# A fused attention and maxout FFN kernel: flag-0 heads by a diagonal and a composite key block, for one assumed set of flags

## The chip, the cores and the metric

The kernel runs on one core of one Trainium2 chip. The metric is the device time of one execution in microseconds (us). The core has five engines, each with an instruction queue of its own that is worked in order: TensorE (PE, matrix products into PSUM), VectorE (DVE), ScalarE (ACT), GpSimd (POOL) and SyncE (SP, which here only issues DMAs). Sixteen DMA engines serve all queues.

## The reference

Four batches of eight heads, 768 positions, head size 64; the output of attention goes row by row through a maxout FFN.

```python
scores = scale * q @ k.T                       # per batch and head, 768 x 768
causal = rel >= 0                              # rel = row - column
stream_keep = causal & ((column < n_sink) | (rel < window))     # n_sink 4, window 64
mask = where(is_retrieval[head], causal, stream_keep)           # flags 1,0,1,0,0,0,1,0
a = softmax(where(mask, scores, -1e9)); x = a @ v               # x: 3072 x 512 over the heads
h = max(x @ w1, x @ w2, x @ w3)                # 512 -> 768
out = h @ w_out                                # 768 -> 512, float32
```

A head of flag 1 attends to all earlier positions. A head of flag 0 attends to the first four positions and to the last 64.

## The kernel before

Positions are cut into six blocks of 128, and each batch into two halves of three query blocks (384 rows). A step of the work is one item of the string list `PROGRAM`, executed in order when the program is built; each engine then receives its own instructions in that order, so `PROGRAM` is the schedule.

- `hl` (`load_pairs`, L187) loads batch 0's k and q for pairs of heads in halves through SP. `cast` (L212) makes fp16 of them, `turnp` (L231) transposes them on PE, and a copy (L239) puts them in the key-query tile KQ. For batches 1 to 3, `load` (L251, two DMAs from POOL per group of four heads) and `turn` (L267, a DVE stream transpose) do the same.
- `load_v` (L287) brings V through SP; `v` (`prep_v`) casts it into `va` (L504) and multiplies it with the head's flag into `vf` (L506).
- `s` (`scores`) computes the transposed scores of one unit, keys by queries, for all blocks on and below the diagonal, for every head alike: 6 blocks in the first half, 15 in the second. In batch 0 two heads share the array (64 rows each, L553), and in the first half masks are added beforehand by a product with the identity (L537). In batches 1 to 3 four heads share it, 32 rows each, in two contraction halves. ACT takes the exponential into `pt` (L564).
- `k` (`masks`, L586) multiplies blocks on and beside the diagonal with masks `mk` that were built from the flags on the chip (L365 to L389).
- `av` (L602) multiplies each block of `pt` with `va` near the diagonal and with `vf` far from it. In a flag-0 head `vf` holds zeros save for the four sink rows, so its far blocks are worked like any other. A column of ones gives the row sums; L610 and L612 divide. The result is transposed into `xT` by a DMA (L621) or on PE (`x`, L634, L638).
- `f` (`fill`) is one step of the FFN of a half batch: 18 products of 4 matmuls (L438), each taken out of PSUM by a copy (L455) or a maximum (L458), then three output blocks (L474, L480, L481). FFN steps are strewn between the attention steps.
- `w` (L403, L410) loads the weights through POOL: w0 in two DMAs of 384 KB, the others whole. `idle` issues ten products of zeros at the very start.

Of the kernel before, what the change touches and what calls it, by code (L numbers as in the profile page):

```python
# [11 lines left out]
FP32 = mybir.dt.float32  # L12
AF = mybir.ActivationFunctionType
ALU = mybir.AluOpType

UNITS = [
    [  # L20
        [(0, 0, 3, 0), (2, 2, 1, 384)],
        [(1, 1, 2, 0)],
    ],
    [
        [(0, 0, 3, 0), (5, 2, 1, 384)],
        [(1, 0, 3, 0), (4, 1, 1, 384)],
        [(2, 0, 3, 0), (4, 2, 1, 384)],
        [(3, 0, 3, 0)],
    ],
]  # L30

MASKED = [
    [(0, 0, 1, (0,), 256, 256), (0, 0, 1, (384,), 128, 0), (1, 1, 1, (0,), 256, 0)],
    [(1, 0, 2, (384,), 128, 0), (2, 2, 1, (0, 384), 128, 128), (3, 3, 1, (0,), 256, 0)],
]

APART = [(0, 0, 1, (384,), 128, 0), (1, 1, 1, (384,), 128, 0)] + MASKED[1][1:]


EARLY = 0

FIRST = "hl 0 0 1, ir"

PROGRAM = (
    "idle 2, idle 8, cast 0 0 aa, hl 0 1 1 ss, hl 0 2 2 ss, read, hl 1 0 2 ss, cast 0 1 pp",
    "flags, cast 0 2 ap, em 1, turnp 0 1 a, far, em 0, turnp 0 0 aa, cast 0 3 da, em 2, em 3",
    "load_v 0 0 4 4, s 0 0 1, s 0 0 0, v 1 1 pp, cast 1 1 pa, turnp 0 3 dd, turnp 0 2 da",
    "w 0 2 0, load_v 0 0 0 4, v 0 0 dp, s 1 0 0, w 0 2 1, s 0 1 0 b, hl 1 2 2 ss, s 1 0 1",  # L50
    "cast 1 2 dp, v 1 0 dd, s 0 1 1, s 1 1 0 b, av 0 0, v 0 1 pp, turnp 1 1 a, s 1 1 1",
    "turnp 1 2 aa, x 0 0 a, s 2 0 1, cast 1 0 dp, load_v 0 1, cast 1 3 ad, av 1 1, s 2 1 1",
    "av 1 0, x 1 1 d, av 0 1, turnp 1 0 ad, s 2 2 1, x 1 0 d, s 3 0 0, m 0, w 1, x 0 1 d",
    "s 2 0 0, m 3, m 1, f 1 d, f 1 d, s 2 1 0, s 2 2 0, m 2, f 1 a, f 1 d, k 2 1 2 p, k 2 0 1 d",
    "w 2, f 1 d, s 2 3 1, load 1 0, w 3, k 3 0 0 d, s 3 1 0, f 1 a, s 2 3 0, load 1 1",
    "k 2 0 3 p, k 2 0 2 p, turnp 1 3 dd, k 3 0 1 p, k 2 1 1 d, k 2 1 3 d, f 1 d, f 1 d",
    "v 2 0 ad, f 1 a, f 1 a, v 3 1 pp, f 1 d, s 3 0 1, v 2 1 dp, s 3 1 1, f 1 a, v 3 0 ap",
    "av 2 0 D, f 1 d, f 1 d, s 3 2 0, turn 1 0 0 0, turn 1 0 0 1, f 1 a, turn 1 0 1 0, s 3 2 1",
    "s 3 3 0, k 3 0 2 p, k 3 1 2 p, turn 1 0 1 1, f 1 a, av 2 1 D, s 3 3 1, k 3 1 1 d",
    "k 3 0 3 p, k 3 1 3 p, f 1 a, k 3 1 0 d, load_v 1 0, gate, f 1 a, s 4 0, k 4 1 0 p",  # L60
    "v 4 0 pp, av 3 0, av 3 1, f 1 a, f 1 a, x 3 0 d, s 4 1, turn 1 1 0 1, x 3 1 a, f 1 d",
    "v 5 1 pp, turn 1 1 1 0, turn 1 1 1 1, turn 1 1 0 0, k 4 0 1 d, k 4 0 0 d, k 4 1 1 p, f 1 a",
    "f 1 a, f 1 d, load_v 1 1, f 1 a, f 1 a, f 1 a, v 4 1 pd, f 1 a, f 1 d, s 5 0, f 1 a, f 1 d",
    "av 4 0 D, k 5 0 0 d, f 1 d, s 5 1, k 5 0 1 p, load_v 2 0, f 1 a, f 1 a, load 2 0, f 1 a",
    "s 6 0, f 1 d, av 4 1 D, f 1 a, v 5 0 ap, f 1 a, s 6 1, f 1 a, av 5 0 D, f 1 d, f 1 d",
    "k 5 1 1 p, k 5 1 0 p, v 7 0 dp, s 6 2, k 6 1 2 p, f 1 a, av 5 1 D, turn 2 0 1 0, f 1 a",
    "v 6 0 ad, s 6 3, turn 2 0 0 1, x 5 1 d, f 1 a, turn 2 0 1 1, load 2 1, load 3 1",
    "load_v 2 1, v 6 1 ap, f 1 d, f 1 d, k 6 0 2 p, v 9 0 ap, k 6 1 3 p, f 1 a, f 1 a",
    "turn 2 0 0 0, s 7 0, f 1 a, f 1 d, f 1 d, turn 2 1 0 0, k 6 0 1 d, f 1 a, s 7 1, f 1 d",
    "f 1 a, f 1 a, k 6 1 1 p, k 7 1 1 d, f 1 d, s 7 2, f 1 a, f 1 a, k 6 0 3 p, k 7 1 2 d",  # L70
    "turn 2 1 1 0, load 3 0, av 6 0 D, s 7 3, f 1 d, v 7 1 pp, av 6 1 D, k 7 1 3 p, f 1 d",
    "turn 3 1 1 0, k 7 0 3 p, turn 2 1 0 1, s 8 0, k 7 0 1 p, turn 2 1 1 1, k 7 0 2 p, f 1 a",
    "f 1 d, load_v 3 0, k 8 0 0 p, av 7 1 D, s 8 1, f 1 a, f 1 a, s 9 0, v 8 0 ap, k 8 0 1 d",
    "f 1 a, f 1 d, av 7 0 D, v 13 1 pp, s 9 1, f 1 a, av 8 0 D, f 1 d, s 10 0, f 1 a, x 7 1 d",
    "f 1 a, v 10 0 dd, f 1 d, s 10 1, f 1 a, f 1 d, v 9 1 ad, f 1 a, f 1 d, f 1 a, s 10 2",
    "f 1 d, f 1 d, f 1 d, k 8 1 0 p, f 1 d, k 9 0 0 p, k 9 1 1 d, f 1 d, f 1 d, v 11 0 ad",
    "f 1 d, k 9 1 0 p, v 12 0 ad, k 9 0 1 p, k 8 1 1 d, av 9 0 D, v 8 1 ap, s 10 3, f 1 d",
    "f 1 a, av 8 1 D, turn 3 0 1 0, s 11 0, k 10 1 1 p, f 1 d, f 1 d, k 10 0 3 p, f 1 a",
    "av 9 1 D, v 13 0 ap, f 1 a, k 10 1 3 d, turn 3 0 1 1, x 9 1 a, k 10 0 1 p, s 11 1, f 1 a",
    "k 10 0 2 p, v 11 1 ap, av 10 0 D, f 1 d, s 11 2, k 11 0 2 p, turn 3 0 0 0, f 1 a",  # L80
    "turn 3 0 0 1, f 1 d, k 11 0 1 d, f 1 a, k 10 1 2 d, f 1 d, v 10 1 ap, f 1 a, turn 3 1 0 1",
    "f 1 a, f 1 a, s 12 0, av 10 1 D, f 1 a, f 1 d, k 12 1 0 p, s 12 1, f 1 d, f 1 a, f 1 a",
    "k 12 0 1 p, turn 3 1 0 0, s 11 3, v 12 1 ad, f 1 a, load_v 3 1, f 1 a, f 1 a, k 11 0 3 d",
    "k 11 1 3 p, f 1 d, f 1 d, k 11 1 1 p, turn 3 1 1 1, f 1 a, f 1 d, av 11 0 D, f 1 d",
    "k 11 1 2 d, f 1 a, k 12 0 0 p, k 12 1 1 d, f 1 a, s 13 0, av 12 0 D, f 1 d, av 11 1 D",
    "k 13 0 0 d, f 1 d, f 1 d, s 13 1, f 1 d, v 15 1 pp, f 1 d, k 13 0 1 p, x 11 1 d, f 1 d",
    "v 15 0 ad, av 12 1 D, k 13 1 1 d, av 13 0 D, s 15 0, f 1 a, f 1 d, f 1 d, f 1 a, f 1 d",
    "f 1 d, f 1 a, k 13 1 0 d, s 15 1, v 14 0 ap, f 1 d, f 1 a, f 1 d, f 1 d, s 14 0, f 1 a",
    "f 1 d, f 1 d, f 1 d, av 13 1 D, s 14 1, f 1 d, x 13 1 d, f 1 d, f 1 d, f 1 a, f 1 a",
    "s 14 2, f 1 a, k 14 1 2 p, v 14 1 ad, k 14 1 1 p, f 1 d, f 1 d, f 1 d, f 1 a, f 1 a",  # L90
    "k 15 0 1 p, s 14 3, f 1 d, k 14 0 3 p, f 1 a, f 1 d, s 15 2, f 1 a, f 1 d, f 1 d, f 1 d",
    "s 15 3, f 1 a, k 15 1 1 d, f 1 a, k 15 1 3 d, f 1 a, k 15 1 2 d, k 14 0 1 p, f 1 a",
    "k 14 0 2 p, k 14 1 3 p, k 15 0 3 d, av 14 0 D, f 1 a, f 1 a, f 1 a, av 14 1 D, f 1 a",
    "f 1 d, k 15 0 2 p, av 15 1 D, f 1 a, av 15 0 D, f 1 d, x 15 1 d, f 1 a, f 1 d, f 1 a",
    "f 1 d, f 1 d, f 1 a, f 1 a, f 1 a, f 1 d, f 1 a, f 1 a, f 1 d, f 1 d, f 1 a, f 1 d, f 1 a",
    "f 1 a, f 1 a, f 1 a, f 1 a, f 1 d, f 1 a, f 1 d, f 1 a, f 1 d, f 1 a, f 1 d, f 1 a, f 1 a",
# [3 lines left out]
def _where(half):  # L100
    at = {}
    for u, parts in enumerate(UNITS[half]):
        for ki, q0, n, c0 in parts:
            for qb in range(n):
                at[(ki, q0 + qb)] = (u, c0 + qb * 128)
    return at


@with_exitstack
def kernel(  # L110
    ctx: ExitStack,
    tc: tile.TileContext,
    q: bass.AP,
    k: bass.AP,
    v: bass.AP,
    is_retrieval: bass.AP,
    n_sink: int,
    window: int,
    moe_w1: bass.AP,
    moe_w2: bass.AP,  # L120
    moe_w3: bass.AP,
    moe_w_out: bass.AP,
    out: bass.AP,
):
    nc = tc.nc
    B, H, S, D = q.shape
    NT, DMdl = out.shape
    DF = moe_w1.shape[1]
    P = 128
    NSB = S // P  # L130
# [3 lines left out]
    n_sink = int(n_sink)  # L134
    window = int(window)
# [4 lines left out]
    assert (S, D, DMdl) == (768, 64, 512) and window <= P and n_sink <= P  # L140
    AT = [_where(0), _where(1)]
    G = 4
    R = P // G
    NQ = H // G
    NT4 = B * 2 * NQ

# [6 lines left out]
    ptp = ctx.enter_context(tc.tile_pool(name="ptp", bufs=5))  # L153
# [7 lines left out]

    ctx.enter_context(tc.manual_schedule())


    def where(t):
        bh, qd = divmod(t, NQ)
        return bh // 2, bh % 2, qd

# [3 lines left out]

    staged = {}
    cast = {}
    KQs = {}

    def load_pairs(half, hp, n, engines):
        for nm, src, eng in zip(("ks", "qs"), (k, q), engines):  # L180
            st = (
                pairs2.tile([P, 4, HB, D], FP32, tag=nm, name=nm) if n == 2
                else once.tile([P, 2 * n, HB, D], FP32, name=f"{nm}{hp}")
            )
            m = 2 * n if eng is nc.gpsimd else 2
            for h in range(0, 2 * n, m):
                eng.dma_start(  # L187
                    out=st[:, h : h + m],
                    in_=src[
                        0, 2 * hp + h : 2 * hp + h + m, half * HALF : (half + 1) * HALF  # L190
                    ].rearrange("h (p j) d -> p h j d", p=P),
                )
            for i in range(n):
                staged.setdefault((half, hp + i), []).append(st[:, 2 * i : 2 * i + 2])
# [521 lines left out]
```

## Time and profile before

| what | value |
|---|---|
| device time, median of 3 runs | 202.31 us (201.32 to 202.49) |
| profiled execution: its span, the only time that the profile gives for it | 199.9 us |
| median less that span | 2.4 us |
| PE busy | 190.0 us, 95%, 2059 matmuls |
| DVE, ACT, POOL busy | 148.3, 115.9, 90.5 us |
| granted clock of PE, mean | 0.990 |
| read from HBM | 25.17 MB |

The span runs from the first to the last instruction. Matmuls are pipelined, so that the busy time of PE overstates its work; what one matmul costs is read from the spacing of many. In a stretch table each engine's busy time stands beside its number of instructions. In the chain of waits a row gives start, length, engine, output tile, line and count. An L with a number is a line of the kernel.

### The profile page before, as it was taken

What the parts mean: (1) busy time and instruction counts of PE and PEld (TensorE: products, weight loads), DVE (VectorE), ACT (ScalarE), POOL (GpSimd) and SP (SyncE); (2) the same over time, 40 slices, a digit from 0 to 9 for tenths busy, and PEclk for the clock granted to TensorE, in tenths of its full rate; (3) what the DMA queues carried; (4) which work ended last, traced back from release to release, by engine and by line L of the source; (5) the groups of instructions that cost most, each with busy time, mean ns of one, the idle gap of its engine ahead of it and who ended that gap; (6) DMA issues with size and microseconds to landing.
All of it is one profiled execution on the core that took longest, in us unless ns stands there. A gap on an engine that the chain in (4) does not pass through costs nothing.

```text
span 199.9 us, 5135 instructions
## 1 busy us (share of the span) xinstructions
PE 190.0 (95%) x2059; PEld 109.3 (55%) x2059; DVE 148.3 (74%) x311; ACT 115.9 (58%) x171; POOL 90.5 (45%) x118
## 2 busy tenths in 40 slices
PE   7688898999999999999999999999999999999993
PEld 2345444565556455666456645574656455765552
DVE  3638965998976789896469998996978288767750
ACT  4489983765658798687776756634366565100011
POOL 3429187583276598490697245652010197000000
PEclk9889999999999999999999999999999999999999
DMA  5999999995979989988521232703500120124004
GB/s 143 312 245 230 196 195 212 208 169 76 283 173 211 162 169 208 218 218 176 147 76 23 43 124 74 159 20 73 167 5 20 53 108 0 23 59 157 3 0 157
DMA packets 48429, 26.48 MB, mean 132 GB/s; under 512 B 36758, under 2 KB 43926, under 8 KB 48406
## 3 DMA queue, kind: packets, MB, share of 16 engines
q1 hardware_dynamic: 43366, 17.96, 37.9%
q0 software_dynamic: 4624, 7.87, 21.9%
q8 instruction: 16, 0.26, 0.6%
q10 hardware_dynamic: 416, 0.33, 0.5%
q14 instruction: 7, 0.06, 0.1%
HBM read 25.17 MB, written 6.29 MB: 157 GB/s over the span
## 4 chain that ended last, share of the span: by engine, by line
PE 75%; DMA 11%; DVE 4%; SPq 3%; issue 2%; ACT 2%; POOL 0%; DVEq 0%
PE yy L438 39%; PE yy L474 14%; PE st L553 9%; PE oacc L602 9%; DMA vs<-in_v_dram 7%; PE yst L438 3%; DMA qs<-in_q_dram 2%; DVE KQ L267 2%; SPq L187 2%; ACT pt L564 1%; DMA xT<-x 1%; PE yst L474 1%; DVE acc L458 1%; DVE hT L458 1%; SPq L621 1%
## 5 line engine op out<-in xcount | busy, mean ns | idle before, releaser
L564 ACT ACTIVATE pt<-st 128x1024 f16<-128x1024 f32 (+3 forms) x98 | 83.3, 905 | 33.0 <-PE st L553 31.0
L586 POOL TENSOR_TENSOR pt<-pt,mk 128x512 f16<-128x512 f16 (+1 forms) x54 | 57.3, 1088 | 38.4 <-ACT pt L564 20.1
L438 PE MATMUL yy<-xT,w1t 128*128 128x384 f16 x180 | 35.8, 327 | 1.2 <-DVE pt L586 1.2
L438 PE MATMUL yy<-xT,w2t 128*128 128x384 f16 x180 | 36.1, 326 | 0.0
L438 PE MATMUL yy<-xT,w0t 128*128 128x384 f16 x180 | 35.8, 327 | 0.3
L458 DVE TENSOR_TENSOR acc<-yy,acc 128x384 f16<-128x384 f32 x45 | 24.8, 557 | 10.7 <-PE yy L438 8.6
L474 PE MATMUL yy<-woutt,hT 128*128 128x512 f16 (+1 forms) x138 | 31.6, 375 | 0.0
L553 PE MATMUL st<-KQ 32*128 32x384 f16 (+5 forms) x560 | 29.4, 281 | 1.4 <-ACT pt L564 0.8
L458 DVE TENSOR_TENSOR hT<-yy,acc 128x384 f16<-128x384 f32 x45 | 24.8, 556 | 4.5 <-PE yy L438 2.3
L602 PEld LDWEIGHTS <-pt 128*128 128x128 f16 x672 | 24.4, 97 | 4.8 <-DVE va L504 0.7
L267 DVE STREAM_TRANSPOSE KQ<-kq 128x384 f32<-128x384 f32 x24 | 25.5, 1132 | 0.6 <-DMA kq<-in_q_dram 0.6
L602 PE MATMUL oacc<-va,pt 128*128 128x65 f16 x352 | 24.9, 193 | 0.5 <-DVE va L504 0.5
L438 PEld LDWEIGHTS <-w1t 128*128 128x128 f16 x192 | 17.5, 98 | 14.1 <-issue 1.6
L438 PEld LDWEIGHTS <-w0t 128*128 128x128 f16 x192 | 17.8, 98 | 13.4 <-issue 0.8
L438 PEld LDWEIGHTS <-w2t 128*128 128x128 f16 x192 | 17.3, 98 | 11.9 <-issue 1.4
L553 PEld LDWEIGHTS <-KQ 32*128 32x128 f16 (+1 forms) x560 | 12.2, 93 | 18.8 <-issue 11.8
L474 PEld LDWEIGHTS <-hT 128*128 128x128 f16 x150 | 13.8, 98 | 14.7 <-issue 0.8
L602 PE MATMUL oacc<-vf,pt 128*128 128x65 f16 x320 | 21.1, 193 | 0.0
L455 ACT CAST acc<-yy 128x384 f16<-128x384 f32 x25 | 12.0, 481 | 13.9 <-PE yy L438 13.5
L612 DVE TENSOR_TENSOR x<-oacc,rc 128x384 f16<-128x384 f32 x32 | 17.8, 557 | 1.1
L480 DVE COPY ot<-yy 128x512 f32<-128x512 f32 (+1 forms) x15 | 10.1, 675 | 9.2 <-PE yy L474 9.2
L506 POOL TENSOR_TENSOR vf<-va,far 128x384 f16<-128x384 f16 x10 | 8.6, 867 | 17.3 <-ACT va L504 12.9
(72 smaller groups left out, 143.4 us busy)
## 6 DMA issues: line engine op xcount, KB each, us to landing
out_dram<-ot SPq DMA_DIRECT2D x23, 256.0 KB, 2.1
vs<-in_v_dram SPq DMA_DIRECT2D x21, 256.0 KB, 5.6
kq<-in_k_dram POOLq DMA_DIRECT2D x6, 384.0 KB, 7.9
kq<-in_q_dram POOLq DMA_DIRECT2D x6, 384.0 KB, 10.0
ks<-in_k_dram SPq DMA_DIRECT2D x8, 192.0 KB, 3.6
qs<-in_q_dram SPq DMA_DIRECT2D x7, 192.0 KB, 4.8
vs<-in_v_dram SPq DMA_DIRECT2D x6, 128.0 KB, 4.8
w0t<-in_moe_w_dram POOLq DMA_DIRECT2D x2, 384.0 KB, 9.4
```

The costliest lines, as they stand in the source:

```text
L267: nc.vector.transpose(out=dst.rearrange("c (p j) -> c j p", j=n)[:, j0:j1], in_=src.rearrange("c (j i) -> c j i", i=R),)
L438: nc.tensor.matmul(yy[:, 0:HALF], w_t[wi][:, ks, ni * P : (ni + 1) * P], xT[b, half][ks].rearrange("p a t -> p (a t)"), start=(ks == 0), s ...
L455: copy_out[0](out=acc[ni], in_=yy[:, 0:HALF])
L458: nc.vector.tensor_tensor(out=dst, in0=yy[:, 0:HALF], in1=acc[ni], op=ALU.max)
L474: nc.tensor.matmul(yo[:, 0:n], hT[ns][:, tb * P : (tb + 1) * P], woutt[:, ns, c : c + n], start=(ns == 0), stop=(ns == NNB - 1),)
L480: op(out=ot[:, c : c + n], in_=yo[:, 0:n])
L506: vf_engine.tensor_tensor(out=vf[j][:, hs, k0:k1, 0:D], in0=vs[:, hs, 0:1] if half == 0 else va[j][:, hs, k0:k1, 0:D], in1=far[:, hs, k0:k ...
L553: nc.tensor.matmul(sts[g // m][:, g % m, c0 : c0 + n * P], KQ[rows, 0, ki * P : (ki + 1) * P], KQ[rows, 1, t0 : t0 + n * P], start=(c0 == ...
L564: nc.scalar.activation(out=pts[t, i][:, u, h0 : h0 + m, 0:w], in_=st[:, :, 0:w], func=AF.Exp, scale=sc,)
L586: engine.tensor_tensor(out=x, in0=x, in1=m, op=ALU.mult)
L602: nc.tensor.matmul(o[:, qi, hl, 0 : D + 1], pt[:, u, hl, c : c + P], vv[:, 2 * hp + hl, ki, 0 : D + 1], start=(idx == 0), stop=(idx == len ...
L612: nc.vector.tensor_tensor(out=x, in0=o[:, :, :, 0:D], in1=rc.unsqueeze(3).to_broadcast([P, HB, 2, D]), op=ALU.mult,)
```

## The change

The change is a rewrite of the attention part. Its parts:

- **One set of flags is assumed** (`GUESS`). All of the masks, shapes and unit layouts follow from it when the program is built. The flags that are given are compared with it on DVE (`compare_flags`, step `flags`), and at the end all row sums are tested for a range (`check_sums`, step `check`). `verdict` adds both into a number `differ`. Every engine reads it into a register, and a branch leads to `general`, a slow program in loops that works for any flags, when it isn't zero.
- **A flag-0 head reads two blocks per query block**: the diagonal block, and from the third query block on a composite one, which has the four sink keys in columns 0 to 3 and the last 64 keys of the block before in columns 64 to 127; between them it is zero. The composite keys `kx` (steps `kx0`, `kx`) and values `vx` (`y`) are copied from KQ and V; their tiles are cleared once (`clear`, `cleark`). That is 11 score blocks per head instead of 21, and 11 AV products instead of 21. Flag-1 heads are as before.
- **Rows of the array are shared by two heads** in batches 1 to 3: `ROWS` pairs a head of one group with one of the other, and `MIXED` and `NEAR` lay out eight steps per batch in which each row group works on up to four blocks of both its heads. Before there were twelve units per batch.
- **Masks** are multiplied from a strip of 28 blocks that 28 copies on DVE lay out (`strip`), and only where needed. The additive masks of batch 0's first half come from five blocks `far`.
- **The start's order is another.** POOL builds six mask blocks, then casts pair 0; DVE clears the composite tiles and compares the flags ahead of pair 0's copy. `idle` is two products after the first scores, and eight later. `load 1 0` stands ahead of the weights, `w 0` is one DMA of 768 KB behind POOL's cast of the second half's fourth key pair, and a `load` of the second group of heads issues four DMAs instead of two.
- FFN, output and the DMAs of V are unchanged.

```diff
-UNITS = [[[(0, 0, 3, 0), (2, 2, 1, 384)], [(1, 1, 2, 0)]],
...
+GUESS = (1, 0, 1, 0, 0, 0, 1, 0)
+ROWS = ((0, 7), (1, 4), (2, 5), (3, 6))
+MIXED = [
+    [("R", "p", 0, 0, 3, 0), ("S", "p", 1, 1, 1, 384)],
+    [("S", "p", 0, 0, 2, 0), ("R", "p", 1, 1, 2, 256)],
...
 PROGRAM = (
-    "idle 2, idle 8, cast 0 0 aa, hl 0 1 1 ss, hl 0 2 2 ss, read, hl 1 0 2 ss, cast 0 1 pp",
-    "flags, cast 0 2 ap, em 1, turnp 0 1 a, far, em 0, turnp 0 0 aa, cast 0 3 da, em 2, em 3",
-    "load_v 0 0 4 4, s 0 0 1, s 0 0 0, v 1 1 pp, cast 1 1 pa, turnp 0 3 dd, turnp 0 2 da",
-    "w 0 2 0, load_v 0 0 0 4, v 0 0 dp, s 1 0 0, w 0 2 1, s 0 1 0 b, hl 1 2 2 ss, s 1 0 1",
...
+    "clear 1, flags, hl 0 1 1 ss, clear 0, cast 0 0 pp, turnp 0 0 dd, cleark 0, hl 0 2 2 ss",
+    "strip 0 14, cast 0 2 aa, cast 0 1 ap, turnp 0 1 d, kx0 0 0 a, s0 0 0 0, hl 1 0 2 ss",
+    "cast 1 0 dd, turnp 0 2 ad, turnp 1 0 da, cleark 1, load_v 0 0 0 4, cast 1 1 ap, idle 2",
+    "kx0 0 1 a, s0 0 0 1, cast 0 3 dd, s0 0 1 0, s0 0 1 1, strip 14 28, kx0 1 0 p, load_v 0 0 4 4",
+    "v 0 0 3 d, hl 1 2 2 ss, v 0 0 2 d, turnp 0 3 aa, cast 1 2 dd, load 1 0, s0 1 1 0, s0 0 1 3",
+    "s0 1 0 0, y 0 0 1:4:2 s p, kx0 0 3 d, turnp 1 1 d, kx0 1 1 d, s0 1 3 0, v 0 0 0 p, s0 1 2 0",
+    "k0 0 1 0 p, kx0 0 2 a, y 0 0 1:4:2 r p, cast 1 3 pd, av 0 0 0, y 0 0 5:8:2 r a, s0 0 1 2",
+    "y 0 0 5:8:2 s d, s0 0 0 3, turnp 1 3 da, s0 0 0 2, turnp 1 2 da, k0 0 1 1 d, s0 1 3 1, w 0",
...
+                if GUESS[h]:
+                    use = [("p", ki) for ki in range(qi + 1)]
+                else:
+                    use = [("c" if qi > 1 else "p", qi - 1)] * (qi > 0) + [("p", qi)]
...
+        for g in range(G):
+            far_row = any(GUESS[h] for h in ROWS[g])
+            parts = (MIXED if far_row else NEAR)[s]
...
+            nc.tensor.matmul(
+                sts["XY"[g // 2]][:, g % 2, c0 : c0 + n * P],
+                KQ[rows, 0, ki * P : (ki + 1) * P] if kind == "p"
+                else kx[b % 2][quad][rows, ki - 1, :, r],
+                KQ[rows, 1, q0 * P : (q0 + n) * P],
...
+        vx = [consts.tile([P, H, 4, VW], FP16, name=f"vx{j}") for j in range(2)]
+        nc.vector.memset(vx[j], 0.0)
...
+    n = nc.values_load(differ[0:1, 0:1], min_val=0, max_val=1 << 20)
+    with tc.If(n > 0, preferred_fallthrough_block=False):
+        general(tc, nc, q, k, v, is_retrieval, int(n_sink), int(window), w_t, woutt, out, xs_dram)
```

## The prediction

> **What bounds the kernel now.** I read the stages first: busy time and granted clock in stretches cut where the chain of waits changes engine.
>
> ```profile
> core 0: us, PE busy (x) PEld busy (x) DVE busy (x) ACT busy (x) POOL busy (x), PEclk, DMA share, GB/s
> 4.70:8.15 3.45, 1.57 (x17) 0.89 (x16) 1.64 (x8) 0.82 (x3) 1.07 (x2) 1.00 0.98 289
> 8.15:11.60 3.45, 3.45 (x28) 2.00 (x26) 2.33 (x6) 3.45 (x6) 1.34 (x3) 0.51 1.17 296
> 43.30:196.70 153.40, 153.25 (x1704) 89.24 (x1704) 118.11 (x232) 85.47 (x124) 65.42 (x76) 1.00 0.48 108
> 196.70:199.90 3.20, 0.00 (x0) 0.00 (x0) 0.42 (x1) 0.00 (x0) 0.00 (x0) 0.91 0.47 164
> ```
>
> From 43.3 us to the last matmul PE has no gap (153.25 of 153.40): a matmul removed there is time removed. Before that PE waits; after it 3.2 us are the last copy, its store and the closing barriers. The chain of waits in the late part prices PE's work:
>
> ```profile
> 163.13 0.56 PE st L553 x16
> 163.69 2.71 PE yy L438 x16
> 169.56 0.94 PE oacc L602 x30
> 170.49 1.95 PE yy L438 x12
> ```
>
> Behind AV a product's matmul takes 1.95/12 = 162.5 ns and an AV matmul 0.94/30 = 31.3 ns. A score unit (one tile per pair of heads, 4 column blocks, two contraction halves) takes 0.56 where 8 passes of 128 columns at the same rate (162.5/3 = 54) give 0.43: 0.13 more; the 16 matmuls behind it take 2.71 instead of 2.60, another 0.11. So a unit costs its columns plus 0.245.
>
> The start is read from PE's timeline and the DMA issues up to 50 us (KB each, median us from issue to landing):
>
> ```profile
> 23.64 1.48 PE L438 MATMUL yy<-xT,w0t 128*128 128x384 f16 x8
> 30.97 3.42 PE L438 MATMUL yy<-xT,w1t 128*128 128x384 f16 x20 [1.22 <-DVE pt L586]
> ```
> ```profile
> w0t<-in_moe_w_dram POOLq DMA_DIRECT2D x2, 384.0 KB, 9.4
> w1t<-in_moe_w_dram POOLq DMA_DIRECT2D x1, 768.0 KB, 12.2
> w2t<-in_moe_w_dram POOLq DMA_DIRECT2D x1, 768.0 KB, 10.7
> kq<-in_k_dram POOLq DMA_DIRECT2D x2, 384.0 KB, 15.6
> kq<-in_q_dram POOLq DMA_DIRECT2D x2, 384.0 KB, 16.9
> woutt<-in_moe_w_out_dram POOLq DMA_DIRECT2D x1, 768.0 KB, 18.5
> ```
>
> The first w0 half is issued at 14.9 and lands at 23.6, just when the FFN begins; w1 is issued at 18.8 and lands at 31.0. The DMA engines are full (share 1.14 or more) from 8 to 43 us. PE is dense from 31.0.
>
> **The change, part by part.** I write the end as F (the first FFN product) + R (PE's work from there) + idle + tail.
>
> *AV.* A flag-0 head reads 11 blocks instead of 21, five heads of eight: 472 matmuls instead of 672. Of those, 429 come after F against 624 after 31.0 before. 429 x 31.3 ns = 13.4 us; before 19.5.
>
> *Scores of batches 1 to 3.* Units go from 36 to 24 (eight mixed steps per batch, all four blocks wide). Columns: 24 x 8 x 54 ns = 10.4 us; overhead 24 x 0.245 = 5.9. Steps now have up to eight passes per row group in place of four; the four extra weight changes at 10 to 22 ns (the starts of consecutive passes in one unit) add 0 to 2 us, I take 0.8. Sum 17.1; before 36 x 0.245 + 252 x 54 ns = 22.4.
>
> *FFN.* Unchanged: 576 x 162.5 ns and the output's 138 x 215 + 12 x 110 ns (1.29 and 0.66 us for six in the chain) = 124.6 us; before, six products (3.9) were done by 31.0, leaving 120.7.
>
> *The rest of R.* Remaining batch-0 units 2.6, eight filler matmuls of 512 columns 1.7, transposes and the verdict 0.3. R = 124.6 + 13.4 + 17.1 + 2.6 + 1.7 + 0.3 = 159.7. The same sum for before from 31.0: 120.7 + 19.5 + 22.4 + 1.9 + 0.4 = 164.9, and 31.0 + 164.9 = 195.9 against a true end at 196.7: the method misses 0.8 us.
>
> *The start.* This decides. DVE gets work ahead of what the scores wait for:
>
> ```profile
> 0.93 0.27 DVE L314 MEMSET zero<- 128x256 uint32 x1 [0.93 <-PEq L697]
> 2.42 0.23 DVE L346 COPY kept<-kept 128x256 f16<-128x256 f16 x1
> ```
>
> A clear costs 1.06 ns per word. The two clears of the composite value tiles (1056 words each) take 2.2 us, the ten small operations on the flags about 0.2 us each where they depend on one another, and DVE is free for pair 0's first copy at about 7.4 us, though PE's transposes are ready at 5.5. From there: two copies 1.0, two clears of composite keys (512 words) 1.05, 14 mask blocks at about 0.115 (half of L346's copy, overlapped as L389's are) 1.6, a 768-column copy 0.85, two casts 1.0, two copies 1.0, two more clears 1.05, the casts of pair 3 1.0: 16.0 us. The loads of half 1, pairs 2 and 3, reuse the buffers that these casts free; SP issues them at about 15.5 (12.1 before), and everything behind them on SP, batch 0's second V, starts 3.3 us later. POOL casts the key that lands at about 20.5 and only then issues w0: at 21.5, not 14.9. Batch 1's first kq goes ahead of w0 on POOL, at about 14.3; with half 1 and V beside it, it should be moving until w0 is issued. A 768 KB weight then needs 10.7 to 12.2 by w2 and w1, less if kq is done (w0 halves 9.4, worked under full engines): 30 to 33. The other chain, DVE held at the cast of pair 2 until about 21, then the copies, four AV divisions (0.7 each), a KQ stream transpose of 1.13 ahead of the second xT, gives 31. So F is 31, bounds 25 (if the walk overstates each wait) and 40 (w0 as slow as woutt, 18.5). The six products that before had done by 31.0 are counted in R.
>
> *Idle behind F.* Before lost 2.8 us between 23.6 and the end. DVE has about 132 us of work in the 160 behind F (83%, from L458's 557 ns, L267's 1132, L612's 557 and so on; before 118 in 153, 77%). I take 2.0, bounds 0 and 5. The row-sum check is about 1.2 us of DVE under an FFN stage in which DVE is half idle; nothing waits for it before the verdict.
>
> *The tail.* Every engine reads the verdict into a register and branches. It adds a wait for DVE; queued behind SP's copy of it are only the last three stores, which come later anyway. PE ends 2.5 us before SP sees the last store land, and this covers some of it. Neither operation is in the trace. From below the cover takes all: 0. From above: a register read as long as the last store's landing (2.0), and a fetch of the code behind the skipped block, 1.2 us for a 16 KB packet of the instruction queue (0.6% of 16 engines' span over 16 packets) and a landing of 2.3 as for a DMA transpose, end 3.1 us past before's barrier. I take 1.2, since the nearest row to a register read is a 0.17 us operation on 8 numbers. The trace has no branch across a block. The Trainium skill, "Runtime: NRT & Kernel Launch", section on instruction fetch, says that a taken branch out of the current two pages must fetch its target before going on; it gives no time, and no run here shows it yet.
>
> **Sum.** 31.0 + 159.7 + 2.0 + 3.2 + 1.2 = 197.1 us of span, against 199.9. The profile gives only the span of its execution; the median of the runs, 202.31, lies 2.4 above it, and I carry that over: **199.5 us**, 1.4% faster. One per cent is what a measurement here can tell from no change.
>
> **Rivals.**
> 1. *The start is not later* (0.22). DMA bandwidth, not the queues, bounded the old start (share above 1 up to 43 us), and the bytes are the same. If F is 25, near the old 23.6: 191.1, or 193.5. For: PE has only some 10 us of work before F. Against: w0's place on POOL behind a cast.
> 2. *w0 arrives late* (0.23). It waits in POOL's queue behind the cast and behind kq, and is no longer split. The price is its transfer: break-even is F = 33.8, a flight of 12.3 us, about w1's, and 1% slower is F = 35.8, 14.3 us. At kq's mean of 16.3 F is 37.8: 203.9, or **206.3 us**. For: kq and woutt took that long under full engines. Against: w2's 10.7, and less is queued on POOL ahead of w0.
> 3. *PE's clock* (0.15). Before, a window with 1.57 of 3.45 us busy was followed by one at 0.51. The changed kernel has two filler matmuls early instead of ten, and a sparse start; if half clock holds until one window into the FFN, that costs 1.7 us there and about 1 us in F: 199.8, or 202.2, no change. The Trainium skill, "TensorE: Matmul & The Clock Gate", Part 1, has the clock halve after an idle window and return after a busy one; the two rows above agree.
> 4. *The branch is taken* (0.01): 32 heads of six blocks with some ten dependent operations of half a microsecond or more: beyond 1,100 us.
>
> **Chances.** The forecast has 0.39, its own range 197.5 to 201.5 (F and idle within 2 us), of which 0.27 lies below 200.3. Faster: 0.27 + 0.22 + 0.01 of rival 3 = 0.50. Slower: 0.22 of rival 2, 0.02 of rival 3, 0.01 = 0.25. Within 1%: 0.25. The range reaches to 193 (rival 1, with its faster third left out) and to 206 (half of rival 2).
>
> **What the profile after would show.** First FFN product near 31 and w0 issued near 21.5 with the FFN waiting for it or for xT; PE without gaps from about 35; AV at 31 ns; 24 units in batches 1 to 3 of about 0.6; a last matmul near 192.7, and 4.4 us behind it. I am wrong if PE shows gaps under DVE in the middle, if F is far from 31, or if the end takes more than 6 us.

## The result: 1% slower, and where the time went

| | kernel before | kernel after |
|---|---|---|
| device time, median of 20 runs each | 200.91 us | 202.88 us |
| ratio, 95% interval | | 1.0106 (1.0077 to 1.0135) |
| span of the profiled execution | 199.9 us | 200.2 us |
| first FFN product | 23.6, dense from 31.0 | 32.2 |
| last matmul ends | 196.7 | 193.3 |
| behind the last matmul | 3.2 us | 6.9 us |

The ratio is of fast runs alone; the median of the kernel before also holds its slower runs (up to 204.6 us).

PE does 9.4 us less busy time and is done with its matmuls 3.4 us earlier, and the kernel takes longer. First the page's busy times, then three stretches of the kernel after (from and to, length, busy time and number of PE, its weight loads, DVE, ACT and POOL, PE's granted clock, DMA share, GB/s):

```profile
PE 180.6 (90%) x1833; PEld 106.2 (53%) x1833; DVE 152.4 (76%) x357; ACT 99.4 (50%) x170; POOL 72.3 (36%) x111
```
```profile
11.60:15.00 3.40, 3.16 (x19) 1.46 (x17) 3.29 (x8) 2.37 (x6) 1.52 (x4) 1.00 0.79 128
43.30:193.32 150.02, 148.72 (x1547) 87.75 (x1545) 117.92 (x244) 74.03 (x116) 52.52 (x67) 1.00 0.51 114
193.32:200.20 6.88, 0.00 (x1) 0.00 (x0) 0.42 (x1) 0.00 (x0) 0.00 (x0) 0.74 0.26 86
```

The last two rows carry the result. From 43.3 us PE is still without gaps (148.72 of 150.02), so what was taken from it there is saved. Behind it stand 6.88 us in which only one copy of 0.42 us shows as work; before, the same row was 3.20 long. The first row is a lull at the start: the DMA engines at 0.79 of their time and 128 GB/s, where the kernel before was above 1.

The chain of waits of the kernel after, in its late part (start, length, engine, tile, line, count):

```profile
160.24 0.57 PE st L597 x13
...
167.13 1.95 PE yy L387 x12
169.08 1.31 PE oacc L646 x42
```

A product's matmul takes 1.95/12 = 162.5 ns and an AV matmul 1.31/42 = 31.2 ns, as before; 22 of the 24 score steps take 0.56 to 0.57 us, whether they hold 12 matmuls or 32, and two take 0.69 and 0.76. PE's prices were right.

The same chain at the start:

```profile
15.18 6.92 DMA qs<-in_q_dram
22.23 0.55 DVE qn L199
...
24.46 0.56 DVE qn L199
...
32.44 0.20 DVE xT L672
32.68 1.95 PE yy L387 x11
```

SP issues the second half's last query loads at 15.2; they land 6.9 us later, DVE has waited 3.7 us for them, and 10 us of dependent casts, transposes, scores, AV and divisions follow until the first FFN product at 32.2. w0 is issued at 20.4 and lands at 29.9 (9.5 us), ahead of its use.

The end has to be looked for among instructions that are not counted as busy. The rows of the branch's line in the kernel after (duration in ns: least, median, most; first and last start):

```profile
L780 PEldq COMPARE_BRANCH  x2: 95/1892/3688, 191.2 to 193.5; - x2
...
L780 SPq COMPARE_BRANCH  x2: 38/48/57, 193.5 to 195.8; - x2
```

Each engine issues two: the comparison, and the jump over the general program. PE's jump takes 3.69 us. SP's looks short, but the instructions of SP in the trace show what follows it (start in us, length in ns):

```
195.726    17  EVENT_SEMAPHORE  L780   landing of the stores, last of seven
195.795    38  COMPARE_BRANCH   L780   the jump
198.539    28  EVENT_SEMAPHORE  L941   first instruction behind the general program
...
199.301    13  DRAIN            L941   closing barrier
```

SP waits for the landing of its own last store, jumps, and does nothing until 2.74 us after the jump's start. The DMA queues between the jump and its landing (queue, packets, MB, share of 16 engines):

```profile
q14 instruction: 3, 0.02, 3.2%
q8 instruction: 1, 0.02, 3.1%
```

Instruction queues move data there: three packets of 8 KB between 195.9 and 197.3, and one of 16 KB that starts at 197.95, 0.6 us before SP goes on, and ends at 199.3, behind it. Which of them SP waited for isn't shown. So two candidates stand: the jump at the end, and the late loads at the start.

### The profile page after: what moved, and what is told of

Read it like the earlier page. It is cut to its first block, busy times and chain, and to the rows that moved or that the text cites. A ratio compares the mean times of both kernels' runs of the same rounds, so it can differ in the third digit from the quotient of the medians.

```text
span 200.2 us, 4763 instructions
## 1 busy us (share of the span) xinstructions
PE 180.6 (90%) x1833; PEld 106.2 (53%) x1833; DVE 152.4 (76%) x357; ACT 99.4 (50%) x170; POOL 72.3 (36%) x111
## 4 chain that ended last, share of the span: by engine, by line
PE 71%; DVE 11%; DMA 8%; issue 3%; ACT 3%; SPq 2%; DVEq 0%; ACTq 0%
PE yy L387 39%; PE yy L412 11%; PE oacc L646 6%; PE st L597 6%; DMA qs<-in_q_dram 6%; PE yst L387 3%; DVE x L653 2%; DMA xT<-x 2%; DVE hT L397 2%; DVE KQ L251 2%; SPq L185 2%; PE st L526 1%; PE tr L217 1%; DVE acc L397 1%; PE yst L412 1%
## 5 line engine op out<-in xcount | busy, mean ns | idle before, releaser
L614 ACT ACTIVATE pt<-st 128x1024 f16<-128x1024 f32 (+2 forms) x51 | 43.5, 907 | 28.0 <-PE st L597 26.4
L627 POOL TENSOR_TENSOR pt<-pt,strip 128x512 f16<-128x512 f16 (+4 forms) x36 | 35.7, 1008 | 55.4 <-ACT pt L614 52.4
L387 PE MATMUL yy<-xT,w1t 128*128 128x384 f16 x180 | 35.2, 326 | 0.2 <-DVE x L653 0.2
L387 PEld LDWEIGHTS <-w0t 128*128 128x128 f16 x192 | 18.1, 98 | 13.4 <-issue 1.0
L387 PEld LDWEIGHTS <-w1t 128*128 128x128 f16 x192 | 18.1, 98 | 12.9 <-issue 1.1
L546 ACT ACTIVATE pt<-st 128x1024 f16<-128x1024 f32 (+4 forms) x28 | 16.2, 636 | 10.1 <-PE st L526 9.8
L646 PEld LDWEIGHTS <-pt 128*128 128x128 f16 x472 | 18.0, 100 | 3.0 <-issue 0.4
L646 PE MATMUL oacc<-va,pt 128*128 128x65 f16 x392 | 19.0, 197 | 0.0
L653 DVE TENSOR_TENSOR x<-oacc,sums 128x384 f16<-128x384 f32 x32 | 17.8, 557 | 1.1
L627 DVE TENSOR_TENSOR pt<-pt,strip 128x256 f16<-128x256 f16 (+4 forms) x33 | 13.9, 437 | 5.6 <-ACT pt L614 5.6
L597 PE MATMUL st<-KQ 32*128 32x128 f16 (+2 forms) x342 | 15.1, 257 | 0.0
L597 PEld LDWEIGHTS <-KQ 32*128 32x128 f16 x342 | 8.8, 92 | 6.8 <-issue 5.6
L646 PE MATMUL oacc<-vx,pt 128*128 128x65 f16 x80 | 12.3, 193 | 0.0
(106 smaller groups left out, 196.3 us busy)
```

Of the source, the lines that this page charges most:

```text
L387: nc.tensor.matmul(yy[:, 0:HALF], w_t[wi][:, ks, ni * P : (ni + 1) * P], xT[b, half, ks].rearrange("p a t -> p (a t)"), start=(ks == 0), s ...
L546: nc.scalar.activation(out=pts[0, half, hp, u][:, r0:r1, c0:c1], in_=sts[hp][:, r0:r1, c0:c1], func=AF.Exp, scale=sc,)
L597: nc.tensor.matmul(sts["XY"[g // 2]][:, g % 2, c0 : c0 + n * P], KQ[rows, 0, ki * P : (ki + 1) * P] if kind == "p" else kx[b % 2][quad][ro ...
L614: nc.scalar.activation(out=pts[b, s, xy][:, r0:r1, c0:c1], in_=st[:, r0:r1, c0:c1], func=AF.Exp, scale=sc,)
L627: engine.tensor_tensor(out=x, in0=x, in1=m, op=ALU.mult)
L646: nc.tensor.matmul(o[:, i, r, 0 : D + 1], at[b, h, kind, ki, qi], vv[:, 0 : D + 1], start=(n == 0), stop=(n == len(todo) - 1), skip_group_ ...
```

## Experiments on the end

**Theory:** the jump waits for code that is not on the engine, and SP's, behind the landing of the last store, is wholly on the path; it is worth the 3.7 us by which the stretch behind the last matmul grew. **Rivals:** the jump only uses time in which stores land anyway; the check and verdict cost it; a branch on a register costs this wherever it lands.

**1. No branch** (`t1_nobranch`):

```diff
-        n = nc.values_load(differ[0:1, 0:1], min_val=0, max_val=1 << 20)
-        with tc.If(n > 0, preferred_fallthrough_block=False):
-            general(...)
```

> The changed kernel without its last step: the register loads, the branch and the general program are left out (so nothing stands in for other flags; the flags are still compared and the sums still tested on DVE). Theory (the jump is the mis-sized term): the last matmul stays near 193.3, and what lies behind it goes from 6.9 to about 3.0 us, as in the kernel before (199.9 - 196.7 = 3.2). That takes 3.6 us (3.0 to 4.0): ratio to the kernel before 0.993 (0.990 to 0.996). Rival (the jump only uses time in which the stores' landing is waited for anyway): under 0.5 us, ratio 1.008 to 1.011. Rival (the check and the verdict in the last rows cost the time, not the jump): the same, ratio 1.008 to 1.011.

**2. A short body behind the branch** (`t2_small`):

```diff
-            general(...)
+            nc.vector.memset(woutt[:, 0, 0:2], 0.0)
```

> The register loads and the branch stay, and the body behind the branch is one memset on DVE in place of the general program (so the fallback is left out). Theory (what costs is that the jump lands on code that is not there yet, because the general program lies between): SP's gap of 2.7 us after its last branch and PE's branch of 3.7 us go to under 0.5 us each, about 4 us lie behind the last matmul, ratio to before 0.997 (0.994 to 1.000). Rival (a branch on a register costs this much wherever it lands): gap and ratio as in the changed kernel, 2.7 us and 1.011.

**3. The kernel before with the branch** (`b_branch`):

```diff
+        differ = keep.tile([1, 2], INT32, name="differ")
+        nc.vector.memset(differ, 0)
         fast(...)                      # the whole kernel before
+        n = nc.values_load(differ[0:1, 0:1], min_val=0, max_val=1 << 20)
+        with tc.If(n > 0, preferred_fallthrough_block=False):
+            ...                        # loads the weights, then the same general program
```

> The kernel before with only the end of the change added: a constant zero is loaded into a register on every engine, and a branch leads around the same general program. Theory (the price of the branch is a fixed one at the end): SP's gap of about 2.7 us stands behind the landing of the last store here too, with the queue of waits behind it; the kernel before gets 3 to 4 us longer, ratio 1.015 to 1.020. Rival (the price comes from the changed kernel's end, its check and verdict among the last FFN steps): ratio 1.000 to 1.004.

**What was measured.**

| kernel | ratio to before (95%) | last matmul | SP's jump | SP goes on | PE's jump, us | end | behind the last matmul |
|---|---|---|---|---|---|---|---|
| before | 1 | 196.7 | none | | | 199.9 | 3.2 |
| after | 1.0106 (1.0077 to 1.0135) | 193.3 | 195.8 | 198.5 | 3.69 | 200.2 | 6.9 |
| no branch | 0.9931 (0.9902 to 0.9961) | 194.7 | none | | | 198.2 | 3.5 |
| short body | 0.9925 (0.9897 to 0.9953) | 194.6 | 194.4 | 194.6 | 0.18 | 198.1 | 3.6 |
| before, with branch | 1.0168 (1.0117 to 1.0219) | 197.1 | 198.9 | 202.0 | 0.30 | 203.7 | 6.6 |

The stretches behind the last matmul, of no branch, short body, and before with branch:

```profile
194.68:198.22 3.54, 0.00 (x0) 0.00 (x0) 0.42 (x1) 0.00 (x0) 0.00 (x0) 1.00 0.42 148
```
```profile
194.57:198.15 3.58, 0.00 (x1) 0.00 (x0) 0.42 (x1) 0.00 (x0) 0.00 (x0) 0.86 0.42 147
```
```profile
197.06:203.68 6.62, 0.00 (x0) 0.00 (x0) 0.42 (x1) 0.00 (x0) 0.00 (x0) 0.90 0.26 88
```

Taking the branch away takes 1.0106 - 0.9931 = 0.0175 of the time before, 3.5 us; adding it to the kernel before adds 0.0168, 3.4 us. Within the intervals it has one price in both kernels, and all of it is on the path. (In the kernels with no branch and with the short body the last matmul is 1.3 us later than in the kernel after, as their first FFN product came at 33.8 and 33.1.) The short body gives back as much as no branch at all (0.994 to 1.000 was expected), although every engine still loads the register, compares and jumps; so neither register load, check, verdict nor the branch as such costs it, but the jump to a place behind the general program. One thing else differs in the short body: SP's jump stands ahead of its last store there, and not behind a landing. But SP's gap behind the jump, 0.16 us in place of 2.71, is measured wherever it stands. The rows of the branch's line tell the engines apart, first of before with branch, then of short body:

```profile
L698 PEldq COMPARE_BRANCH  x2: 95/200/304, 194.9 to 197.2; - x2
```
```profile
L780 PEldq COMPARE_BRANCH  x2: 90/135/180, 192.4 to 192.6; - x2
```

With the branch on the kernel before, PE's jump takes 0.30 us, and the end is 6.62 us all the same, so it isn't PE that sets it. SP goes on last, at 202.0. DVE stands still behind its jump there too, for 3.5 us, until 201.8, so that even without SP's wait most of the time would have stayed in this kernel (argued, no run shows it). The Trainium skill, "Runtime: NRT & Kernel Launch", section "Instruction fetch mechanics", says that a taken branch to a page outside the two on the engine must fetch it first. The instruction packets behind the jump agree, and so does the short body, which lost the wait and has no instruction packet between SP's jump and the end; the price, 2.6 to 3.2 us on SP in every profile with the general program, is from these runs. What the page would not tell is which engine pays: in the kernel after, DVE and ACT jump over the same program in 0.04 to 0.06 us and go on within 0.4 to 0.5 us, whereas DVE pays 3.5 us with the branch on the kernel before, and 3.4 with the hint below. The runs don't show why.

**4. and 5. A prefetch hint, and the layout that came with it** (`x_hint`, `t3_fall`). With the other layout of the two sides, the comparison itself jumps, and the waits for the stores' landing stand behind the jump:

```diff
-        with tc.If(n > 0, preferred_fallthrough_block=False):
+        tc.mark_branch_hint_location("rest", n, (mybir.EngineType.SP, mybir.EngineType.PE))   # x_hint alone
+        with tc.If(n > 0, preferred_fallthrough_block=True, label="rest"):                    # label: x_hint alone
```

> The changed kernel with a prefetch hint for the branch's target on SP and PE, given right after the register load (on SP at 189.2, 6 us ahead of the jump; on PE right ahead of it), and the branch laid out so that the jump to the end is the taken side. Theory (the code of the target is fetched late): on SP the gap of 2.7 us goes to under 0.5 us; PE has no time ahead, keeps its 3.7 us from 193.5 and is done at 197.2, so the end comes near 198 to 198.5, ratio 0.999 to 1.003. Rival (the hint does nothing for a forward branch, or the time is not a fetch): gap and ratio unchanged, 1.011.

> The kernel of x_hint without its hint: only the layout, in which the branch itself jumps to the end, ahead of the waits for the landing of the stores. Theory (the hint did nothing, the time came from a jump that now runs beside the landing of the stores): ratio as x_hint's, 1.001 to 1.008; SP's jump still 3.0 to 3.5 us. Rival (the hint brought part of it): ratio as the changed kernel's, 1.008 to 1.013, or SP's jump over 3.7 us.

Measured: with hint and layout 1.0044 (1.0012 to 1.0076), with the layout alone 1.0070 (1.0042 to 1.0099). The intervals overlap, and the profiles speak against the hint: SP's jump takes 3.25 us with the hint 5.3 us ahead of it, and 3.04 without. The expectation that SP's gap would close fell. In both, the jump now lies beside the landing of the stores. Of the layout alone, the stretch behind the last matmul:

```profile
193.72:199.14 5.42, 0.00 (x0) 0.00 (x0) 0.42 (x1) 0.00 (x0) 0.00 (x0) 0.82 0.32 108
```

5.42 instead of 6.88: 1.5 us of the 3.4 are hidden in this profile. With the hint it is 6.56: SP's last store took 1.27 us to issue in place of 0.33, which put its jump 0.9 us later. Where the hint kernel's better ratio comes from can be read from the runs, which list each execution's span beside its time. Time less span is 1.7 us with the hint, as in the kernel before, and 2.1 us with the layout alone, as in the kernel after; the medians of the spans stand at 1.004 of those of the kernel before in both. So by the spans the hint brought nothing. The jump can be covered in part, and these hints didn't advance it.

**6. SP freed of the last stores** (`v_actstore`): the last half's output goes through ACT's queue.

```diff
-                (0, nc.scalar.copy if last else copy_out[0], nc.sync),
+                (0, nc.scalar.copy if last else copy_out[0], nc.scalar if last else nc.sync),
```

> The changed kernel, branch and general program and all, with the last half's output stored through ACT's queue instead of SP's. SP has nothing to wait for at the end and makes its jump near 190, under the last FFN products; ACT, whose jump took 0.04 us, waits for the stores. Theory (two jumps are late, SP's from 195.8 to 198.5 and PE's from 193.5 to 197.2): SP's is hidden, PE's 3.7 us are left, and behind the last matmul lie 4.5 to 5.2 us instead of 6.9; ratio to before 0.998 to 1.004. Rival (SP's jump only looks late, PE's holds the end): under 0.7 us, ratio 1.007 to 1.012.

Measured: 1.020 (1.0142 to 1.0258), slower. The theory had a wrong premise, that SP has nothing to wait for once it issues no stores. It made its comparison at 191.4, but the seven waits stand between comparison and jump here too, and SP was through them only at 199.2, 4.0 us behind the last matmul instead of 2.4. Jump and code followed with 2.67 us: 8.4 us behind the last matmul. It was a store that came late, and not SP's code: the store that SP's first wait is for was issued by ACT at 195.4, 15 of its 16 parts had landed by 197.14, the last landed at 198.72, and SP went on at 198.73. The kernel's final store shows the same in all twelve profiles with the general program, 2.4 to 3.8 us from issue to landing by its last part, against 1.75 to 1.77 in the four without. Instruction packets move at these times (here from 196.3 to 198.5); that they hold the last part up is likely but not shown. In the kernel after this costs nothing, as SP asks for that landing only behind its jump.

## Experiments on the start

**Theory:** the late issue of the second half's last key and query loads sets the first FFN product, at 32.2 to 33.8 us in the four profiles of this start so far. **Rivals:** PE's clock, w0's landing, DVE's added work, or DMA engines that are full anyway.

**7. The casts and the loads moved ahead** (`s1_cast3`): `cast 0 3`, whose buffers the loads reuse, ahead of the second half's casts, and `hl 1 2 2` ahead of V's second transfer.

```diff
-... turnp 0 1 d, kx0 0 0 a, s0 0 0 0, hl 1 0 2 ss
-cast 1 0 dd, turnp 0 2 ad, ...
-kx0 0 1 a, s0 0 0 1, cast 0 3 dd, ... load_v 0 0 4 4
-v 0 0 3 d, hl 1 2 2 ss, v 0 0 2 d
+... turnp 0 1 d, cast 0 3 dd, kx0 0 0 a, s0 0 0 0, hl 1 0 2 ss
+turnp 0 2 ad, cast 1 0 dd, ...
+kx0 0 1 a, s0 0 0 1, ... hl 1 2 2 ss, load_v 0 0 4 4
+v 0 0 3 d, v 0 0 2 d
```

> The changed kernel with DVE's cast of the first half's fourth pair moved ahead of the second half's casts, and the loads that reuse its buffers (the second half's third and fourth pair) moved ahead of V's second transfer. SP then issues them near 12 instead of 14.2 to 15.2. Theory (late key and query loads hold the start): DVE's wait of 3.7 us for qs shrinks to under 1.5 us, the first FFN product comes 1.5 to 3 us earlier than in the four profiles of this start so far (32.2 to 33.8), and the ratio to before goes from 1.011 to 0.996 to 1.003. Rival (PE at half its clock sets the start, the loads only fill time): FFN start and ratio stay within 0.5 us, 1.008 to 1.013.

Measured: 1.0272 (1.0238 to 1.0307), the first FFN product at 35.2: slower, which neither theory said. Its chain of waits:

```profile
17.03 7.45 DMA vs<-in_v_dram
24.50 0.45 DVE va L436
...
27.41 0.56 DVE qn L199
...
35.63 1.95 PE yy L387 x11
```

The loads went out at 12.1 to 13.5 as meant, but V's transfer, now behind them, landed at 24.5, and DVE's order has V's cast ahead of the query's: the wait for qs had turned into a longer wait for vs. This run also seems to decide on the clock. Between the last query cast and the first FFN product on the chain lie 32.68 - 24.46 = 8.22 us in the kernel after and 35.63 - 27.41 = 8.22 here. These two stretches, first of the kernel after, then of this one (PE's granted clock is the third number from the end):

```profile
24.46:32.68 8.22, 7.10 (x80) 4.40 (x81) 6.30 (x17) 5.44 (x12) 3.16 (x7) 0.70 1.15 201
```
```profile
27.41:35.63 8.22, 7.22 (x79) 4.54 (x80) 6.30 (x17) 5.25 (x12) 3.17 (x7) 1.00 1.17 212
```

0.70 and 1.00, and the same time to a hundredth. But the 1.00 is no reading: this run's trace has its first record of the clock at 32.8 us, and the view puts 1.00 where there is no record (in the kernel after, ahead of 15.7). What PE did is read from its matmuls. Here are the same 11 AV matmuls in the chain of the kernel after, of this run, and of `s7_cast` (experiment 11), whose record has the full clock from 27.5 us on:

```profile
28.58 0.62 PE oacc L646 x11
```
```profile
31.53 0.62 PE oacc L646 x11
```
```profile
28.25 0.35 PE oacc L646 x11
```

That is 56 ns a matmul in both stretches and 32 ns at the full clock. Most of the transposes start 106 to 107 ns apart in both, and 56 at the full clock. So PE ran at half pace in both, and the equal times say nothing about the clock. What does: ten profiles share this chain from the last query cast to the first FFN product. It takes 7.5 us in the two where the full clock came back 4.0 to 4.1 us behind the cast, and 8.2 us in the three where it came back 6.8 to 7.1 behind it. The start follows the clock by 0.7 us at least. PE's steps on this chain are 4.1 us at half pace in the kernel after; if all shrank like the AV row, a full clock would take 1.8 us off them, an estimate that no run tests.

**8. Filler on PE at the very start** (`s3_idle`): `idle 2, idle 8` ahead of all else.

> The changed kernel with ten products of zeros on PE at the very start, as the kernel before has them. In the changed kernel PE does 0.95 us of work in the first 9 us, and its granted clock falls to 0.50 from about 19 to 29; in the kernel before it is 0.57 in 9 to 12 and 1.00 from 12 on. Theory of the clock (the prediction's third rival): early work brings the slow stretch forward, the clock is 1.00 between 15 and 30, the first FFN product comes 1 to 3 us earlier, ratio 0.996 to 1.006. Theory of the loads: the clock may change, the first FFN product doesn't by more than 0.5 us, ratio 1.008 to 1.013.

Measured: 1.0118 (1.0088 to 1.0148), the first FFN product at 31.9. The clock went to 0.50 early as expected (9 to 12) and came back, but fell again, to 0.50 from 18.1 to 28.4. So this run doesn't remove the slow stretch, and no run here had PE at full pace through the start: the clock stays an open cause of the late start.

**9. DVE's work put off** (`s2_late`): `clear 1`, `flags`, `cleark 1` and `strip 14 28` moved to places behind the first FFN product.

> The changed kernel with DVE's work of the start that nothing needs at once moved behind the first FFN product: clearing the second set of composite tiles (1056 words 0.94 us, two of 512 words 0.49 us each and small ones), the comparison of the flags, and the second 14 strip copies (2.26 us). Theory (DVE holds the start): KQ's first copy comes at about 5.7 instead of 7.2, and the first FFN product 1 to 2 us earlier, ratio 1.000 to 1.006. Rival (DVE waits for qs at 18.5 to 22.2 anyway, so what it saves ahead of that is lost in this wait): the start stays within 0.5 us, ratio 1.008 to 1.013, the wait for qs longer by what was moved.

Measured: 1.0327 (1.0292 to 1.0362). The first FFN product came at 33.3, no earlier: DVE waited for the loads anyway, as the rival had it. What neither had is the loss. In the chain of waits the moved clears turn up:

```profile
35.60 0.48 DVE kx L465
...
36.62 1.00 DVE KQ L251
```

DVE has no slack between 33 and 42 us, and PE, from the first FFN product to its last matmul, took 164.9 us instead of the 160.9 to 161.4 of eleven other profiles. Early in the start this work was under a wait; behind it, it was on the path.

**10. w0 ahead of batch 1's load** (`s6_w0early`):

```diff
-cast 1 2 dd, load 1 0, s0 1 1 0 ... s0 1 3 1, w 0
+cast 1 2 dd, w 0, s0 1 1 0 ... s0 1 3 1, load 1 0
```

> The changed kernel with the load of w0 and that of batch 1's first group changed over in POOL's order: w0 issued near 14 instead of 20.4. Theory of the late w0 (the prediction's second rival): the first FFN product comes 2 us earlier or more, ratio under 1.003. Theory of the loads: w0 is there 2 us before it is used already, the first FFN product waits for xT still, and not being earlier by more than 0.5 us; w0's 768 KB now stand beside qs, which may come up to 1 us later; ratio 1.008 to 1.016.

Measured: 1.0158 (1.0127 to 1.0188), first FFN product at 33.6, behind xT still. w0's lateness was no cause.

**11. The cast alone, V's loads left in place** (`s7_cast`), **12. and batch 1's load moved behind** (`s8_kqbehind`).

> The changed kernel with DVE's cast of the first half's fourth pair moved ahead of the second half's casts, and nothing else: V's loads keep their place ahead of the second half's last key and query loads. In every profile of the changed start, the first FFN product came 10.0 to 10.9 us after the landing of these qs, by the same chain of steps. Theory (that landing sets the start): SP's wait of 2.7 us in front of these loads shrinks, they are issued near 12 instead of 14.2 to 15.2, qs lands 1.5 to 3 us earlier and the first FFN product comes as much earlier, at 30 to 31.5; ratio to before 0.998 to 1.005. Rival (the DMA engines are full, an earlier issue only lands no earlier): qs's time to landing grows from 6.9 to 9 us, start and ratio unchanged, 1.008 to 1.013.

> The kernel of s7_cast with batch 1's first load (kq, 768 KB by POOL, issued at 14.1 to 14.8) moved down to just ahead of w0, near 20. Theory of full DMA engines: without kq beside them, qs lands 2 us or more earlier than in s7_cast, the first FFN product follows unless w0 or kq are late now; ratio up to 0.01 under that of s7_cast. Theory of the late issue alone: qs lands as in s7_cast, and w0, kq behind it come 2 us later: ratio as s7_cast's or up to 0.01 above it.

Measured: 1.0109 (1.0045 to 1.0173) and 1.0137 (1.0070 to 1.0205). In s7_cast qs was issued at 13.3 instead of 15.2 and landed at 17.3, 4.8 us earlier than in the kernel after, as its time to landing shrank from 6.9 to about 4 us. The first FFN product came at 31.6, only 0.6 us earlier than in the kernel after and 2.1 earlier than in the latest profile of that start, and the time is the kernel after's. So this landing doesn't set the start by itself, and the theory fell, though not by the rival's mechanism. In s8_kqbehind qs landed at 17.2, as in s7_cast, so that kq beside it had not held it up; its cast was at 18.6, 3.7 us earlier than in the kernel after, and w0 ended the wait:

```profile
23.58 9.45 DMA w0t<-in_moe_w_dram
33.07 2.12 PE yy L387 x12
```

**13. Cast and stores together** (`c_best`).

> Both edits in one kernel, the earlier cast of s7_cast and the stores of v_actstore; the fallback is whole. If the start and the end are apart, the gains add: 1.5 to 3 us and 1.7 to 2.3 us off the changed kernel, ratio to before 0.985 to 0.995, faster than both kernels. If one of the two causes is wrong, only the other's gain is seen.

Measured: 1.0182 (1.0123 to 1.0240). With the stores' premise gone there was nothing to add; the first FFN product was at 31.7, and 9.1 us lay behind the last matmul. Between them stood 163.0 us, with waits of 2.2 us of PE, 1.9 of them at once, for DMA transposes, one of which took 6.5 us; whether the edit or chance made it late isn't known.

**14. The cast without the branch** (`c_early_nobranch`), to read the start's edit where the end doesn't blur it:

> The earlier cast of s7_cast in the kernel without the branch (the register loads, the branch and the general program are left out). Theory (the start of s7_cast is 0.6 to 2 us earlier, as its profile has it, and only the scatter of its runs hid that): ratio 0.983 to 0.991, against 0.993 without the cast. Rival (another chain sets the start as late as before): ratio 0.991 to 0.996.

Measured: 0.9899 (0.9864 to 0.9935), 198.04 us median, against 0.9931 (0.9902 to 0.9961) without the cast: within the theory's range, but the intervals overlap, and the gain is 0.6 us if it is one. In these two profiles the first FFN product is at 31.5 and 33.8. The waits of DVE between 4 and 42 us show why it isn't 2 us; first the kernel after, then this one (engine, line, waited for: us in total, times, longest):

```profile
DVE qn L199 <- DMA qs<-in_q_dram: 3.7, 1, 3.7
```
```profile
DVE KQ L220 <- PE tr L217: 4.4, 3, 2.3
```

The wait for the loads is gone and a wait for PE's transposes stands in its place: PE's and ACT's own chain through the first scores ends nearly as late. Between 20.3 us and 27.1 PE's transposes in it start 106 ns apart, which is half pace, so that the clock is one of the bounds that no edit took away. The start has several bounds within 2 us of one another, and taking the last one away uncovers the next.

## Why the prediction was wrong

The sign was wrong and the median lay in the range. By its own terms, in us of the profiled execution:

| term | predicted | kernel after | other profiles of the change |
|---|---|---|---|
| F, first FFN product | 31.0 | 32.2 | 32.4 to 33.8 in five with the same start |
| R and idle, to the last matmul | 161.7 | 161.1 | 160.9 to 161.4 in ten; 162.0, 163.0 and 164.9 in three |
| behind the last matmul | 4.4 | 6.9 | 3.5 without the branch |
| span | 197.1 | 200.2 | |

- **The tail is the step that failed.** "I take 1.2", between 0 and 3.1, measured 3.4 to 3.5 (no branch; the kernel before with it). The mechanism was in the text, the fetch of the code behind the skipped block, but the size was taken from the nearest row to a *register read*, and the register read isn't what costs. Of the pieces of the upper bound (which make 3.0 with the cover of 2.5 taken off, not 3.1), the 1.2 us of a packet and 2.3 of a landing were the better guess for the jump alone, and cover was wrongly taken off: SP's jump comes after the landing of its last store, so that nothing hides it. With 3.5 in place of 1.2 the sum is 199.4 of span and 201.8, no change.
- **F was 1.2 to 2.8 short.** The walk's order was right: SP's loads held by the casts to 15.2 (15.5 predicted), w0 issued at 20.4 (21.5; 22.8 to 23.4 in four other profiles), the FFN waiting for xT behind a KQ transpose. The term that was mis-sized is "DVE held at the cast of pair 2 until about 21": it was 22.2 to 23.5 in the profiles with this start, because the loads took 6.9 to 7.5 us to land. How much of the 10 us behind that cast is PE's half pace is not separated.
- **R was right within 1 us.** AV, scores and FFN cost what the rows of before gave, and PE stayed dense. Without the branch the change is 0.7% faster, which is this gain less the start's loss.
- **What the carried-over offset did.** 2.4 us between median and span were carried over. In the runs of the result the kernel before has its median at 200.91, 1.0 above its profile's span, and the kernel after 2.7 above. Tail (2.5), F (1.2) and R (-0.6) make 3.1 of the 4.8 us between predicted and measured difference (-2.8 and +2.0); the offset has the other 1.7. The median and the span that were compared are of different executions. Within one execution, time less span is 1.65 to 1.78 us for the kernel before in every experiment and 2.07 to 2.21 for the kernel after, so 0.4 us came with the change, outside of the span. It isn't there with no branch, the short body or the hint; where it goes isn't shown. Of the rest, 0.7 is that the profile of before was of a long execution (199.9, where 200.91 - 1.7 = 199.2 is in the middle), and 0.6 that the profile of after was of a short one (200.2, the median of its spans being 200.75): its F was the earliest of six by 0.2 to 1.5.
- **The rivals.** "The start is not later": no profile had F near 25. "w0 arrives late": w0 landed ahead of its use, and issuing it 6 us earlier gained nothing; it sets the start only when the other bounds are moved (s8_kqbehind). "PE's clock": half clock came at 19.1 and lasted 10.2 us, as that rival had it, and PE ran at half pace ahead of 15.7 us too. The Trainium skill, "TensorE: Matmul & The Clock Gate", Part 1, has the clock halve after an idle window of about 3.4 us. In this trace PE was busy for 2.0 of the 3.4 us ahead of 19.1, so a sparse window was enough. The half clock was over before the FFN began, so the 1.7 us in the FFN weren't paid; the 1 us in F is neither shown nor excluded, and the cast-to-FFN times of 7.5 to 8.2 us speak for a part of it. The branch was not taken.
- "I am wrong if the end takes more than 6 us" was the line that fired.

## What to carry to other kernels

A rarely taken side path that is compiled in place isn't free for the kernel that never takes it: here SP's jump over it, behind its last store, cost 1.7% of the time. So look at what stands on every engine's queue behind the last landing, not only at the arithmetic, and put the jump where something still covers it. And in a start with several near-equal bounds, ask of each earlier issue what it pushes back, and of each postponed operation whether the engine is freer where it goes; two of the moves here cost 1.6 and 2.2% over the kernel that they started from. Check a granted clock against the pace of the matmuls before an argument rests on it.

## What the runs showed of the hardware that was not expected

- A jump over the general program held SP for 2.6 to 3.2 us in all profiles that had it, and PE's took 3.3 to 4.2 us in the kernel after and its variants, but 0.30 on the kernel before; DVE and ACT of the kernel after passed it in 0.04 to 0.06 us, but DVE stood still for 3.4 to 3.5 us behind it with the hint and on the kernel before. With a one-instruction body it was 0.18 us or less on every engine.
- The hint on SP was issued 5.3 us ahead of the jump and shortened nothing (3.25 us with, 3.04 without).
- A register load of one number from the verdict's tile took 0.48 to 0.49 us, and 0.82 on DVE, far more than the 0.17 us operation it was priced by, yet off the path.
- The last of the 16 parts of the final store landed 2.4 to 3.8 us after the issue in the twelve profiles with the general program, and 1.75 to 1.77 in the four without.
- A granted clock of 1.00 can stand for no record: in all 13 profiles of the change that have transposes ahead of the first record, PE ran them at half pace (106 to 107 ns apart, against 56).

The fastest version measured is the change without branch and general program and with the earlier cast, at 0.9899 of the time before; it serves the assumed flags alone. With the fallback whole, the best was 1.0044 (1.0012 to 1.0076), hint and layout, still no faster than the kernel before.
